# One expert's phi units loaded after its gathered rows and multiplied in its fourth step

## The chip, the cores and the metric

The kernel runs on one core of one Trainium2 chip. The metric is device time in microseconds (us) from the start to the end of one execution. Engines are named as the profile names them: PE (TensorE matmul), PEld (its weight loads), DVE (VectorE), ACT (ScalarE), POOL (GpSimd), SP (SyncE, which issues most DMAs). All data are float32.

## The reference

```python
state = gamma * state + k_t v_t^T; y_t = scale * q_t @ state      # retention, 4 x 8 heads, 768 steps
x = y as (3072, 512)
e_idx = argmax(x @ w_gate, 1)                                      # 8 experts, one for each token
ye = relu(x[mask_e] @ w1[e]) @ w2[e]                               # w1: 512x1024, w2: 1024x512
x = gate_w * sigmoid(x @ w_output_gate)[e] * ye                    # first mixture
logits = x @ phi                                                   # 32 slots
slot_in = softmax(logits, axis 0).T @ x ; slot_out = second mixture(slot_in)
out = softmax(logits, axis 1) @ slot_out
```

## The kernel before

Stage one (lines 312 to 718) computes retention tile by tile, writes the token rows to a DRAM table `xs` (lines 602 and 610) and sorts the tokens into eight lists, one for an expert. The experts are then taken in an order that the data decide; SP reads each expert's number into a register (`load_er`, line 195). Stage two (lines 834 to 1160) takes expert after expert, each in eight steps f of 128 hidden features; g counts all 64 steps. Stage three is the second mixture and the output.

Three streams of weights pass through SP, which issues in program order:

- W1: a step has a unit of 256 KB (`load_w`, line 207, three buffers `r`). ACT rounds it to `wh` (line 221) and DVE takes the rest, `wl` (line 222). In step g the unit of step g+3 is issued and the unit of step g+2 is split.
- phi units: w2 is never multiplied with the hidden rows for the logits; instead `wq_mm` (line 237) forms w2 times phi for an expert, 32 matmuls over four units q of 512 KB (`wq_load`, line 230, tile `wt`), and `wq_turn` (line 244) has DVE transpose the result to `wp`. `logits` (line 902) multiplies `wp` with the hidden rows `h`, first at f = 4 of the expert's own steps.
- `m2`: weights of the second mixture, fetched ahead into 21 places of 1024 columns (pool `m2p`, line 835; `load_m2`, line 1082, in every odd step from g = 5).

The place in question is the passage from stage one to stage two. At its end SP issues three W1 units and the four phi units of the first expert, two to a DMA of 1 MB (lines 677 to 680), into the buffers of stage one's input (`raw`). POOL gathers the first expert's 384 rows, in three DMAs of 128 rows, from `xs` into `xg` (line 704), as soon as the first list stands (lines 692 and 695). PE runs `wq_mm(0)` (line 687) and DVE `wq_turn(0)` into `pd` (line 718). Then every engine reads a number and branches past a block of code for experts with too many tokens (`If`, line 818; in this input the block is skipped). The first instruction after it on DVE is `x_scale(0, 0)` (line 852), which multiplies the gathered rows by their gate; PE transposes them (`x_mm`, line 861), ACT and DVE split the result to `xh` and `xl` (lines 870 and 871), and `l1` (line 883) runs a step: 12 matmuls.

SP's order after the branch is that of the code: the second expert's four phi units, held until the first gather has landed (lines 1049 to 1053), then step by step a W1 unit, m2 and the phi units for the expert after next. `wq_mm(1)` runs in step f = 4 of the first expert (`u = UMM + 2`, line 1094), later experts' in step f = 2.

```python
        for q in range(0, KD, 2):
            wq_load(0, q, 2, io, "raw")                  # 680
        wq_mm(0, pT, "w")                                # 687
        wq_turn(0, pd[:, 0:KF, :])                       # 718
        for q in range(KD):
            get = wq_load(1, q, 1, wup, "wu")            # 1051
            if q == 0:
                after(get, gets[0])
```

Of the kernel before, what the change touches and what calls it, by code (L numbers as in the profile page):

```python
# [9 lines left out]
F32 = mybir.dt.float32  # L10
# [12 lines left out]
E = 8  # L23
FF = 1024
NS = 32
NCH = S // 128
NTILE = NT // 128
KD = DM // 128
KF = FF // 128
# [6 lines left out]
CAP = NT + 256  # L36
NPRE, NX = 42, 4
NH = 6
IO, UMM = 6, 2
GROUPS = [(t, 3) for t in range(0, NTILE, 3)]  # L40
ENDS = {t + n - 1: (t, n) for t, n in GROUPS}
ORDER = "xe sc s m g1 gc xr rr g2 G0 Gb q oq os st G1 rk k".split()
# [95 lines left out]
def retention_moe_kernel(ctx, tc, qt, kt, kn, vn, gates, moe_w1, moe_w2,  # L138
# [50 lines left out]
    pd = per.tile([128, NBX, 32], F32, name="pd")  # L189
# [5 lines left out]
    def load_er(k):  # L195
        if k < E:
            er.append(nc.values_load(ordi[0:1, k:k + 1], engines=[mybir.EngineType.SP], min_val=0, max_val=E - 1))
# [9 lines left out]
    def load_w(g):  # L207
        if g >= G:
            return
        k, f = divmod(g, KF)  # L210
        t = wraw.tile([128, DM], F32, tag="r1", name="r1")
        nc.sync.dma_start(out=t, in_=moe_w1[bass.ds(er[k], 1), f:f + 1].rearrange("o q p c -> (o q p) c"))
        raw_t[g] = t
# [14 lines left out]
    wtt, wacc, wp = {}, {}, {}  # L228

    def wq_load(k, q, n, pool, tag):  # L230
        t = pool.tile([128, n * FF], F32, tag=tag, name="wt")
        get = nc.sync.dma_start(out=t, in_=moe_w2[1, bass.ds(er[k], 1), :, q * FF:(q + n) * FF].rearrange("o p d -> (o p) d"))
        for h in range(n):
            wtt[k, q + h] = [t[:, h * FF + g * 256:h * FF + g * 256 + 256] for g in range(4)]
        return get

    def wq_mm(k, pool, tag):
        wacc[k] = pool.tile([128, 256], F32, tag=tag, name="wps")
        for q in range(KD):
            for g, t in enumerate(wtt.pop((k, q))):  # L240
                nc.tensor.matmul(out=wacc[k][32 * g:32 * g + 32, :], lhsT=phi[:, q, :], rhs=t,  # L241
                                 start=(q == 0), stop=(q == KD - 1), skip_group_check=True)

    def wq_turn(k, out):
        wp[k] = out
        nc.vector.transpose(out=out, in_=wacc.pop(k).rearrange("p (f t) -> p f t", t=32))
# [65 lines left out]
    with ExitStack() as pa:  # L312
        sc2 = pa.enter_context(tc.tile_pool(name="sc2", bufs=2))
        io = pa.enter_context(tc.tile_pool(name="io", bufs=IO + 1))
        one = pa.enter_context(tc.tile_pool(name="one", bufs=1))
        pT = pa.enter_context(tc.tile_pool(name="pT", bufs=1, space=PSUM))
# [54 lines left out]
        raw, k2, q2, sps, sS, Ops, xT3, xr3, gps, gts, gs, scl, gr, oz = ({} for _ in range(14))  # L371
# [304 lines left out]
        load_er(0)  # L676
        for g in range(3):
            load_w(g)
        for q in range(0, KD, 2):
            wq_load(0, q, 2, io, "raw")  # L680
        rank(i)
        lp = pT.tile([128, 32], F32, tag="s", name="lp", bufs=2)
        nc.tensor.matmul(out=lp, lhsT=ones, rhs=base[:, 2, :], start=True, stop=False)
        for u in range(NTILE):
            for a in range(2):
                nc.tensor.matmul(out=lp, lhsT=lrow[:, u, :], rhs=lcol[:, u, a, :], start=False, stop=(a == 1 and u == NTILE - 1))
        wq_mm(0, pT, "w")
        lx = one.tile([128, E, 4, E], F32, name="lx")

        def lists(r):  # L690
            n = r.stop - r.start
            nc.vector.tensor_tensor(out=lx[:, r], in0=lp.rearrange("p (e j) -> p j e", j=4).unsqueeze(1).to_broadcast([128, n, 4, E]),
                                    in1=sq8[:, 0, r, :].unsqueeze(2).to_broadcast([128, n, 4, E]), op=ALU.mult)
            with nc.allow_low_precision(reason="a single whole number under 2 ** 24 among zeros"):
                nc.vector.tensor_reduce(out=xidx[:, r], in_=lx[:, r], axis=AX.X, op=ALU.add)
# [19 lines left out]
        nc.vector.tensor_reduce(out=lim[:, E:E + 1], in_=lim[:, 0:E], axis=AX.X, op=ALU.max)  # L715
        nc.vector.tensor_copy(out=limi, in_=lim)
        lists(slice(1, E))
        wq_turn(0, pd[:, 0:KF, :])

    whl = ctx.enter_context(tc.tile_pool(name="whl", bufs=3))  # L720

# [113 lines left out]
    m2p = ctx.enter_context(tc.tile_pool(name="m2p", bufs=NPRE // 2))  # L835
    hp = ctx.enter_context(tc.tile_pool(name="hp", bufs=NH))
    hbp = ctx.enter_context(tc.tile_pool(name="hbp", bufs=1))
    w2p = ctx.enter_context(tc.tile_pool(name="w2p", bufs=8))
    wup = ctx.enter_context(tc.tile_pool(name="wup", bufs=KD))
    with ExitStack() as pb:  # L840
        sp = pb.enter_context(tc.tile_pool(name="sp", bufs=1))
        ps_h = pb.enter_context(tc.tile_pool(name="ps_h", bufs=2, space=PSUM))
        ps_1 = pb.enter_context(tc.tile_pool(name="ps_1", bufs=1, space=PSUM))
# [173 lines left out]
        def slot_acc(e):  # L1017
            nc.vector.scalar_tensor_tensor(out=acc, in0=acc, scalar=sms.pop(e)[:, 4:5], in1=slo.pop(e), op0=ALU.mult, op1=ALU.add)
# [27 lines left out]
                load_w2(e, (2 * f - 6, 2 * f - 5))  # L1046

        load_er(1)
        for q in range(KD):

            get = wq_load(1, q, 1, wup, "wu")
            if q == 0:
                after(get, gets[0])
        for j in range(len(XT[0])):
            if j == 1:
# [6 lines left out]
        for g in range(G):  # L1062
            e, f = divmod(g, KF)
            if f == 0:
                load_er(e + 2)
            if e + 1 < E and f < len(XT[e + 1]):

                gather(e + 1, (f,))
                if f:
                    after(gets[e + 1][f], [relu[-1]])  # L1070
            split_w(g + 2)
            if e and f == 1:

                if e > 1:
                    slot_acc(e - 2)
                logit_parts(e - 1)
            if g < G - 3:
                load_w(g + 3)
            else:
                load_m2(wraw, "r1")  # L1080
            if g > 3 and g % 2 and len(m2_t) < NPRE:
                load_m2(m2p, "m2", 2)
            if f in (4, 5) and e + 1 < E:
                for j in range(2 * f - 8, min(2 * f - 6, len(XT[e + 1]))):
                    x_scale(e + 1, j)
            if f == KF - 1 and e + 1 < E:

                xps = x_mm(e + 1, "ABDr", sorted(((j, kk) for kk in range(KD) for j in range(len(XT[e + 1]))),
                                                 key=lambda b: XT[e + 1][b[0]] < 128))
                l1(g, lambda: [x_split(e + 1, ps) for ps in xps])  # L1090
            else:
                l1(g)
            behind(e - 1, f)
            u = UMM if e else UMM + 2
            if f == u and e + 1 < E:
                wq_mm(e + 1, ps_1, "A")
                wq_turn(e + 1, sp.tile([128, KF, NS], F32, tag="wp", name="wp", bufs=2))
            if f > u and f <= u + 3 and e + 2 < E:

                for q in ((0, 1), (2,), (3,))[f - u - 1]:  # L1100
                    wq_load(e + 2, q, 1, wup, "wu")
            elif G - 14 < g < G - 6 and f % 2:
                load_m2(wup, "wu", 2)
            if g == G - 6:
                load_w2(e, range(4), xp, "xy")
            if g >= G - 2:

                for i, tag in enumerate(("wh1", "wl1")):
                    load_w2(e, (2 * f - 8 + i,), whl, tag)
            if f == 4:  # L1110
                logits(e, 0)
            if f == 5:

                mask(e)
            if f >= 5:
                h_tr(e, 2 * f - 10)
                h_tr(e, 2 * f - 9)
        e = E - 1
# [30 lines left out]
        for kk in range(KD):  # L1149
            nc.tensor.matmul(out=ps4[:, kk, :], lhsT=acc[:, kk * 128:(kk + 1) * 128], rhs=sw,  # L1150
                             start=True, stop=True, skip_group_check=True)
# [171 lines left out]
```

## Time and profile before

| | |
|---|---|
| median of 3 runs | 437.55 us (435.31 to 442.07) |
| the profiled execution | 435.42 us |
| its span, first to last instruction | 433.6 us, so 1.8 us lie around it |
| mean granted PE clock | 0.948 of full |
| busy: PE, DVE, ACT, POOL | 377.8, 258.4, 162.2, 108.1 us |
| DMA | 130.88 MB, mean 302 GB/s |

Times in the rows are counted from the span's start. In the timeline a row gives start, length, engine, line, operation and tiles, and in brackets how long the engine was idle before and what ended that. SPq, DVEq and so on are the engines' queues of control instructions. Where the chain of waits names a DMA, its time runs from the issue to the landing.

### The profile page before, as it was taken

The page shows a single profiled execution, that of the slowest core. Times are in us where ns is not written, and L with a number is a line of the kernel's source. Part 1 is how long each engine was busy: PE and PEld are TensorE (multiplying, and loading weights), DVE is VectorE, ACT ScalarE, POOL GpSimd, SP SyncE. Part 2 cuts the span into 40 slices and gives each one's busy share as a digit, 9 for nine tenths or more (in the row PEclk, how much of TensorE's full clock was granted, in tenths as well). Part 3 has the DMA queues.
Part 4 walks back from the last instruction along what each step waited for, and adds up shares of the span by engine and source line. Part 5 has one row for each costly group of instructions (what it writes and reads, how often), then busy time and mean ns, then how long its engine had stood idle before and what let it go on. Part 6 is the DMA issues. An engine that isn't in the chain of part 4 may idle for free.

```text
span 433.6 us, 11468 instructions
## 1 busy us (share of the span) xinstructions
PE 377.8 (87%) x4398; PEld 285.2 (66%) x4398; DVE 258.4 (60%) x676; ACT 162.2 (37%) x359; POOL 108.1 (25%) x117
## 2 busy tenths in 40 slices
PE   2989999998335999999999999999999996799990
PEld 2877777786214897778777867877778873224560
DVE  1498889998604365595574765754766756424350
ACT  1432222222012644655454644635454431112242
POOL 2303333321120413143052241421521212020020
PEclk9999999999655999999999999999999999699996
DMA  8999999963587798988978979889577789999998
GB/s 268 381 425 347 288 322 322 324 162 76 119 304 247 238 360 300 381 273 295 390 248 303 380 267 346 298 275 377 166 253 278 257 281 289 390 384 408 397 365 291
DMA packets 66275, 130.88 MB, mean 302 GB/s; under 512 B 10436, under 2 KB 28866, under 8 KB 63650
## 3 DMA queue, kind: packets, MB, share of 16 engines
q1 hardware_dynamic: 59426, 118.07, 78.4%
q0 software_dynamic: 3344, 8.34, 6.3%
q10 hardware_dynamic: 3440, 3.63, 2.5%
q8 instruction: 37, 0.61, 0.6%
q14 instruction: 28, 0.23, 0.2%
HBM read 116.84 MB, written 13.20 MB: 300 GB/s over the span
## 4 chain that ended last, share of the span: by engine, by line
PE 72%; DVE 9%; DMA 7%; issue 4%; ACT 3%; another core or an unknown queue 2%; SPq 1%; ACTq 1%; POOL 0%; DVEq 0%; POOLq 0%
PE hps L883 31%; PE s L414 5%; PE gps L992 5%; PE o L447 4%; PE fh L1176 4%; PE so L1213 3%; PE wps L241 3%; DMA raw<-in_qt_dram 3%; DMA xg<-xs,xidx 3%; PE lps L909 3%; PE xps L861 2%; PE o L438 2%; PE slo L1014 2%; PE st L461 1%
## 5 line engine op out<-in xcount | busy, mean ns | idle before, releaser
L883 PE MATMUL hps<-xh,wh 128*128 128x416 f32 (+2 forms) x256 | 92.0, 360 | 0.1
L883 PE MATMUL hps<-xl,wh 128*128 128x416 f32 (+2 forms) x256 | 88.9, 347 | 0.0
L883 PE MATMUL hps<-xh,wl 128*128 128x416 f32 (+2 forms) x256 | 88.7, 346 | 0.0
L222 DVE TENSOR_TENSOR wl<-r,wh 128x512 fp32r<-128x512 f32 x64 | 43.3, 677 | 43.6 <-ACT wh L221 41.2
L888 ACT ACTIVATE h<-hps 128x416 f32<-128x416 f32 (+2 forms) x64 | 32.7, 511 | 81.6 <-PE hps L883 75.9
L883 PEld LDWEIGHTS hps<-xh,wh 128*128 128x128 f32 x256 | 48.1, 188 | 15.1 <-issue 11.4
L975 POOL DMA_INDIRECT ctok<-ce,xidx x29 | 29.2, 1009 | 99.9 <-DVE ce L972 93.5
L221 ACT ACTIVATE wh<-r 128x512 fp32r<-128x512 f32 x64 | 40.0, 628 | 26.4 <-DMA r<-in_moe_w_dram 13.4
L883 PEld LDWEIGHTS hps<-xl,wh 128*128 128x128 f32 x256 | 48.2, 188 | 0.9 <-DVE xl L871 0.3
L883 PEld LDWEIGHTS hps<-xh,wl 128*128 128x128 f32 x256 | 48.1, 188 | 0.6
L704 POOL DMA_INDIRECT xg<-xs,xidx x29 | 29.9, 1031 | 65.3 <-ACT h L888 42.1
L424 DVE TENSOR_TENSOR sS<-s,csa 128x512 f32<-128x512 f32 x48 | 30.5, 675 | 16.3 <-PE s L414 16.3
L414 PE MATMUL s<-raw 64*128 64x128 f32 x384 | 32.5, 305 | 8.7 <-DMA raw<-in_qt_dram 8.3
L414 PEld LDWEIGHTS s<-raw 64*128 64x128 f32 x384 | 27.1, 204 | 11.5 <-DMA raw<-in_qt_dram 5.5
L895 DVE STREAM_TRANSPOSE hB<-h 128x416 f32<-128x416 f32 (+2 forms) x64 | 34.4, 576 | 0.0
L447 PE MATMUL o<-sS,raw 128*64 128x128 f32 x384 | 27.5, 288 | 0.0
L396 POOL TENSOR_TENSOR k<-raw,cs 128x512 f32<-128x512 f32 x20 | 22.3, 1132 | 17.0 <-DMA raw<-in_qt_dram 14.7
L479 ACT COPY xT<-o 128x512 f32<-128x512 f32 x24 | 13.9, 580 | 32.9 <-PE o L447 32.9
L241 PE MATMUL wps<-wt,phi 128*32 128x256 f32 x256 | 17.4, 414 | 9.0 <-DMA wt<-in_moe_w_dram 7.2
L447 PEld LDWEIGHTS o<-sS,raw 128*64 128x64 f32 x384 | 21.6, 142 | 3.9 <-issue 3.6
L992 PE MATMUL gps<-hB,pd 32*32 32x256 f32 x816 | 20.1, 405 | 3.7 <-DVE pd L946 3.7
L870 ACT ACTIVATE xh<-xps 128x416 fp32r<-128x416 f32 (+2 forms) x32 | 16.0, 513 | 14.8 <-DMA wt<-in_moe_w_dram 8.4
(174 smaller groups left out, 525.2 us busy)
## 6 DMA issues: line engine op xcount, KB each, us to landing
m<-in_moe_w_dram SPq DMA_DIRECT2D x41, 512.0 KB
r<-in_moe_w_dram SPq DMA_DIRECT2D x64, 256.0 KB
w<-in_moe_w_dram SPq DMA_DIRECT2D x64, 256.0 KB
wt<-in_moe_w_dram SPq DMA_DIRECT2D x28, 512.0 KB
m<-in_moe_w_dram SPq DMA_DIRECT2D x36, 256.0 KB
xs<-xr SPq DMA_DIRECT2D x32, 192.0 KB
raw<-in_kt_dram SPq DMA_DIRECT2D x5, 1024.0 KB
raw<-in_kn_dram SPq DMA_DIRECT2D x5, 1024.0 KB
```

The lines of the kernel that those rows point to most:

```text
L221: nc.scalar.activation(out=hi, in_=t, func=ACTF.Copy)
L222: nc.vector.tensor_tensor(out=lo, in0=t, in1=hi, op=ALU.subtract)
L241: nc.tensor.matmul(out=wacc[k][32 * g:32 * g + 32, :], lhsT=phi[:, q, :], rhs=t, start=(q == 0), stop=(q == KD - 1), skip_group_check=True)
L414: nc.tensor.matmul(out=ps[h][:, p, :], lhsT=kq(i, p, 0)[r], rhs=kq(i, p, 1)[r], start=True, stop=True, tile_position=(64 * h, 0), skip_gro ...
L424: nc.vector.tensor_tensor(out=sS[i][:, h], in0=sps.pop((i, h)), in1=con("dm", 128)[:, 4 * h:4 * h + 4, :], op=ALU.mult)
L447: nc.tensor.matmul(out=o_at(i, p, h), lhsT=vals(i, 2 * p + h), rhs=s[:, h, p, :], start=(i % NCH == 0 and n < 4), stop=True, skip_group_ch ...
L704: gets.setdefault(e, []).append(nc.gpsimd.indirect_dma_start(out=t[0:r, :], out_offset=None, in_=xs[:, :], in_offset=bass.IndirectOffsetOn ...
L883: nc.tensor.matmul(out=ps, lhsT=a[:, kk * 128:(kk + 1) * 128], rhs=x[e][kk][:, 0:c], start=(n == 0), stop=(n == 11))
L888: relu.append(nc.scalar.activation(out=hs[g][:, 0:c], in_=ps, func=ACTF.Relu))
L895: nc.vector.transpose(out=hB[e][:, 0:NB[e], f, :], in_=hs[e * KF + f][:, 0:c].rearrange("p (b t) -> p b t", t=32))
L975: put = nc.gpsimd.indirect_dma_start(out=ctok[:, :], out_offset=bass.IndirectOffsetOnAxis(ap=xidx[0:r, e, j:j + 1], axis=0), in_=cn[0:r, j ...
L992: nc.tensor.matmul(out=ps[a][32 * j:32 * j + 32, :], lhsT=pd[q, b, :], rhs=hB[e][q, b].rearrange("p f t -> p (f t)"), start=(i == 0), stop ...
```

## The change

The first expert's phi units leave stage one. They are issued after the branch, one DMA a unit, into four of the m2 places, the first held until the first gather has landed, where the second expert's units stood. The second expert's are issued one a step in the first four steps. `wq_mm(0)` and `wq_turn(0)` stand after the matmuls of step f = 3 of the first expert, `wq_mm(1)` after those of f = 5 (before: f = 4). For later experts the fourth unit is issued with the third, one step earlier. `QA` is 0, so that all four units are taken.

```diff
-        for q in range(0, KD, 2):
-            wq_load(0, q, 2, io, "raw")
         rank(i)
...
-        wq_mm(0, pT, "w")
...
         lists(slice(1, E))
-        wq_turn(0, pd[:, 0:KF, :])
...
-        for q in range(KD):
-
-            get = wq_load(1, q, 1, wup, "wu")
-            if q == 0:
+        for q in range(QA, KD):
+
+            get = wq_load(0, q, 1, m2p, "m2")
+            if q == QA:
                 after(get, gets[0])
...
             behind(e - 1, f)
-            u = UMM if e else UMM + 2
+            if e == 0 and f < KD - QA:
+                wq_load(1, QA + f, 1, wup, "wu")
+            if e == 0 and f == 3:
+                wq_mm(0, ps_1, "A")
+                wq_turn(0, sp.tile([128, KF, NS], F32, tag="wp", name="wp", bufs=2))
+            u = UMM if e else 5
             if f == u and e + 1 < E:
                 wq_mm(e + 1, ps_1, "A")
                 wq_turn(e + 1, sp.tile([128, KF, NS], F32, tag="wp", name="wp", bufs=2))
-            if f > u and f <= u + 3 and e + 2 < E:
-
-                for q in ((0, 1), (2,), (3,))[f - u - 1]:
+            if f in (u + 1, u + 2) and e + 2 < E:
+
+                for q in ((0, 1), (2, 3))[f - u - 1]:
                     wq_load(e + 2, q, 1, wup, "wu")
```

On SP, at the end of stage one, before the change: r1 are the W1 units, wt the phi units, limi the number that decides the branch.

```order
L212 DMA r1_1643<-in_moe_w1_dram 128x512
L212 DMA r1_1645<-in_moe_w1_dram 128x512
L212 DMA r1_1647<-in_moe_w1_dram 128x512
L232 DMA wt_1649<-in_moe_w2_dram 128x2048
L232 DMA wt_1651<-in_moe_w2_dram 128x2048
L727 TENSOR_LOAD limi_81
L818 COMPARE_AND_BRANCH
```

The same place after the change (the lines have moved up by four):

```order
L212 DMA r1_1643<-in_moe_w1_dram 128x512
L212 DMA r1_1645<-in_moe_w1_dram 128x512
L212 DMA r1_1647<-in_moe_w1_dram 128x512
L723 TENSOR_LOAD limi_81
L814 COMPARE_AND_BRANCH
```

The two DMAs of 1 MB are gone from in front of the branch.

On SP, from the first DMA after the branch, before the change: wt_3499 to wt_3505 are the second expert's phi units.

```order
L232 DMA wt_3499<-in_moe_w2_dram 128x1024
L232 DMA wt_3501<-in_moe_w2_dram 128x1024
L232 DMA wt_3503<-in_moe_w2_dram 128x1024
L232 DMA wt_3505<-in_moe_w2_dram 128x1024
L197 TENSOR_LOAD ordi_79
L212 DMA r1_3568<-in_moe_w1_dram 128x512
L212 DMA r1_3593<-in_moe_w1_dram 128x512
L212 DMA r1_3618<-in_moe_w1_dram 128x512
L212 DMA r1_3643<-in_moe_w1_dram 128x512
```

The same place after the change: wt_3477 to wt_3483 are the first expert's units, wt_3563 to wt_3644 the second's.

```order
L232 DMA wt_3477<-in_moe_w2_dram 128x1024
L232 DMA wt_3479<-in_moe_w2_dram 128x1024
L232 DMA wt_3481<-in_moe_w2_dram 128x1024
L232 DMA wt_3483<-in_moe_w2_dram 128x1024
L197 TENSOR_LOAD ordi_79
L212 DMA r1_3546<-in_moe_w1_dram 128x512
L232 DMA wt_3563<-in_moe_w2_dram 128x1024
L212 DMA r1_3573<-in_moe_w1_dram 128x512
L232 DMA wt_3590<-in_moe_w2_dram 128x1024
L212 DMA r1_3600<-in_moe_w1_dram 128x512
L232 DMA wt_3617<-in_moe_w2_dram 128x1024
L212 DMA r1_3627<-in_moe_w1_dram 128x512
```

Four units stand in front of the fourth step's W1 unit as before, but each of the next W1 units now has a phi unit in front of it.

## Rows read from the trace of the kernel before

**Rows 1.** The page, the span in 40 equal slices: PE and DMA in tenths.
```profile
PE   2989999998335999999999999999999996799990
DMA  8999999963587798988978979889577789999998
```
**Rows 2.** The page, the costliest group: busy, mean ns of one, idle before.
```profile
L883 PE MATMUL hps<-xh,wh 128*128 128x416 f32 (+2 forms) x256 | 92.0, 360 | 0.1
```
**Rows 3.** The chain of waits, 117 to 139 us: start, length, what.
```profile
118.24 11.44 DMA xg<-xs,xidx
...
130.16 1.52 SPq L232
...
131.88 5.62 DMA wt<-in_moe_w_dram
...
137.62 0.50 ACT xh L870
```
**Rows 4.** The timeline, 116 to 145 us, engine by engine (PE, DVE, ACT, POOL).
```profile
128.38 1.94 PE L241 MATMUL wps<-wt,phi 128*32 128x256 f32 x16 [1.72 <-SPq L818]
135.30 2.79 PE L861 MATMUL xps<-cs,xg 128*128 128x128 f32 x12 [4.99 <-DVE xg L852]
...
119.42 0.39 DVE L695 TENSOR_REDUCE xidx<-lx 128x28 int32<-128x224 f32 x1
130.38 0.45 DVE L246 STREAM_TRANSPOSE pd<-wps 128x256 f32<-128x256 f32 x1 [10.58 <-PE wps L241]
134.56 0.49 DVE L852 TENSOR_SCALAR xg<-xg 128x512 f32<-128x512 f32 x1 [3.72 <-DVEq L818]
...
141.10 0.49 ACT L888 ACTIVATE h<-hps 128x384 f32<-128x384 f32 x1 [0.81 <-PE hps L883]
143.18 0.49 ACT L888 ACTIVATE h<-hps 128x384 f32<-128x384 f32 x1 [1.07 <-PE hps L883]
...
121.16 1.01 POOL L704 DMA_INDIRECT xg<-xs,xidx  x1 [0.30 <-issue]
```
**Rows 5.** Line 818, the branch: ns min/median/max, first and last start in us.
```profile
L818 SPq EVENT_SEMAPHORE  x9: 17/17/17, 125.8 to 128.6; - x9
...
L818 ACTq EVENT_SEMAPHORE  x2: 17/17/17, 125.3 to 125.4; - x2
...
L818 DVEq EVENT_SEMAPHORE  x2: 21/21/21, 134.3 to 134.4; - x2
L818 ACTq COMPARE_BRANCH  x1: 50/50/50, 119.7 to 119.7; - x1
...
L818 DVEq COMPARE_BRANCH  x1: 72/72/72, 131.0 to 131.0; - x1
```
**Rows 6.** A later gather alone: its issue (POOL's timeline), and queue 0, 165.6 to 167.6.
```profile
163.60 1.01 POOL L704 DMA_INDIRECT xg<-xs,xidx  x1 [4.38 <-ACT h L888]
...
q0 software_dynamic: 74, 0.25, 42.9%
```
**Rows 7.** The chain of waits from 138 us: steps 0 to 4, then wq_mm(1).
```profile
138.16 11.22 PE hps L883 x60
149.38 1.86 PE wps L241 x32
```
**Rows 8.** Stretches of 4 us: busy (x) by engine, granted PE clock, DMA share, GB/s.
```profile
120.00:124.00 4.00, 0.00 (x0) 0.00 (x0) 0.00 (x0) 0.00 (x0) 1.87 (x2) 0.50 0.99 356
...
128.00:132.00 4.00, 1.94 (x16) 0.60 (x16) 0.45 (x1) 0.72 (x1) 1.01 (x1) 0.50 0.37 95
132.00:136.00 4.00, 0.70 (x4) 0.73 (x5) 1.44 (x3) 0.00 (x0) 0.00 (x0) 0.50 0.85 301
136.00:140.00 4.00, 3.93 (x17) 3.23 (x16) 1.94 (x5) 2.38 (x6) 0.00 (x0) 0.62 0.81 283
140.00:144.00 4.00, 4.00 (x25) 4.00 (x24) 1.99 (x4) 2.13 (x5) 1.07 (x2) 1.00 0.51 161
...
156.00:160.00 4.00, 4.00 (x30) 3.73 (x29) 2.30 (x5) 2.39 (x5) 1.09 (x1) 1.00 1.01 392
```
**Rows 9.** Tile r, the W1 units: what ended ACT's and DVE's idle time, us, times.
```profile
  DMA r<-in_moe_w_dram: 13.4, 11
```

More of the change, by code (lines that the diff above doesn't have):

```diff
@@ L38 @@
 NH = 6
-IO, UMM = 6, 2
+IO, UMM, QA = 6, 2, 0
 GROUPS = [(t, 3) for t in range(0, NTILE, 3)]
@@ L238, in wq_mm @@
         wacc[k] = pool.tile([128, 256], F32, tag=tag, name="wps")
-        for q in range(KD):
+        for q in range(QA, KD):
             for g, t in enumerate(wtt.pop((k, q))):
                 nc.tensor.matmul(out=wacc[k][32 * g:32 * g + 32, :], lhsT=phi[:, q, :], rhs=t,
-                                 start=(q == 0), stop=(q == KD - 1), skip_group_check=True)
+                                 start=(q == QA), stop=(q == KD - 1), skip_group_check=True)
     def wq_turn(k, out):
@@ L838, in retention_moe_kernel @@
     w2p = ctx.enter_context(tc.tile_pool(name="w2p", bufs=8))
-    wup = ctx.enter_context(tc.tile_pool(name="wup", bufs=KD))
+    wup = ctx.enter_context(tc.tile_pool(name="wup", bufs=KD - QA))
     with ExitStack() as pb:
@@ L1048, in retention_moe_kernel @@
         load_er(1)
-        for q in range(KD):
-            get = wq_load(1, q, 1, wup, "wu")
-            if q == 0:
+        for q in range(QA, KD):
+            get = wq_load(0, q, 1, m2p, "m2")
+            if q == QA:
                 after(get, gets[0])
```

## The prediction

> **What bounds the kernel now.** I read the page's slices first: PE is at nine tenths nearly everywhere, with a hole of three slices about 108 to 141 us and a weaker tail [rows 1]. Inside the expert loop PE waits for nothing: the costliest matmul group has 0.1 us of idle time before it in 256 instructions [rows 2]. So an edit in the loop costs what it adds to PE, unless transfers fall behind, and what the change can win lies in the hole.
>
> The chain of waits through the hole comes next [rows 3]. From 118.24 it lies on the gathers, 11.44 us until all have landed at 129.68; then on SP and the second expert's phi units, and at 137.62 on ACT's first `xh`. Its last releaser, the phi units, is not to be believed: `xh` needs the transposes, and the timeline has them begin at 135.30, released by DVE's scaling of 134.56 [rows 4]. That scaling has 3.72 us of idle time before it, ended by DVE's own branch, and before that 10.58 us in which DVE stood on `wq_turn(0)`. So the true path before 137.62 is: phi units land, second half of `wq_mm(0)` at 128.38, `wq_turn(0)` at 130.38, branch, scaling, transposes.
>
> The branch by itself: ACT compares at 119.7 and runs its first instruction on the skipping path at 125.3, 5.6 us later; DVE compares at 131.0 and is there at 134.3, 3.3 us [rows 5]. Nothing in the program is waited for in between. ACT's wait falls into a stretch with a DMA share of 0.99, DVE's into one that begins at 0.37 and rises to 0.85 [rows 8]. [...]
>
> **The change part by part.** *What goes at the front.* DVE has nothing left before the branch after the lists, which end at 119.42 + 0.39 = 119.81. With the compare at 120.4 at the latest, 3.3 us and the 0.2 us from 134.4 to 134.56, the first scaling stands at 123.9 instead of 134.56: 10.7 us earlier. With ACT's 5.6 us in place of the 3.3 it stands at 126.2, 8.4 us earlier.
>
> The rows must be there too. Two MB of phi units no longer share the engines with the gathers. A later gather, issued at 163.60 among other traffic, has its packets done by 167.6 at the latest, 4.0 us [rows 6]; the third gather is issued at 121.16 [rows 4], so it lands by about 125.2, and its scaling ends about 125.7. PE starts on the first rows at 124.6 (135.30 is 0.74 us after 134.56) and reaches the third rows only after eight of its twelve transposes, 8/12 of 2.79 = 1.9 us, at 126.5: the third gather is covered. The end of the path, 2.32 us from 135.30 to 137.62, is the same. Bounds: gathers as late as now (129.68) put the third scaling's end at 130.2 and the ninth transpose with `xh` at 130.4, which leaves 7.2 us of gain; a compare 0.2 us earlier, right behind the lists, gives 10.9. I take 10.5 us, near DVE's row, less 0.2 us for five engines branching together.
>
> *What comes on PE.* `wq_mm(0)` now ran in PE's idle time and moves between steps 3 and 4. The row of `wq_mm(1)` at full clock gives 1.86 us for 32 matmuls [rows 7]; the half-clock one takes 1.94 us for 16 [rows 4], so 3.9 us is the upper end. It is 1.9 us, with nothing beside it to hide it. `wq_mm(1)` only changes its step. `wq_turn(0)` waits on DVE for PE as the others do; behind it is `wl` of two steps later: nothing.
>
> *The clock.* It is granted at 0.50 until 136, 0.62 on average to 140, and 1.00 from 140 [rows 8]: PE's stream began at 135.30. After the change it begins at 124.6 without the two bursts of `wq_mm(0)` before it. If the rise comes as long after the start, nothing is lost; from -0.3 to +1.7 us (one step at half clock), I take 0.3 us.
>
> *The new wait on SP.* The first unit waits for the gathers (about 125.2) and for the branches of the other engines. Behind it on SP stand three units, a register load and the fourth W1 unit. Before, from the first unit's issue at 130.16 to the last landing at 137.50 it took 7.34 us [rows 3]; issue at 125.4 gives 132.7 for all four. The W1 unit behind them, 256 KB at 349 GB/s (283 at a share of 0.81, [rows 8]), lands about 133.5 and is split to `wh` by 134.2 and `wl` by 135.0. Steps are 2.08 us apart (141.10 to 143.18), the first took 2.94 us from 138.16 to 141.10 [rows 4, 7]; with `l1` starting at 127.7 step 3 is due at 127.7 + 2.94 + 2 x 2.08 = 134.8. So it is just in time, and phi itself is not needed before 136.9.
>
> Then each step asks for a W1 unit, a phi unit and a gather, 0.26 + 0.52 + 0.27 = 1.05 MB, 3.0 us at 349 GB/s against a step of 2.08. From the first unit (126) to the second expert's last there are 6.2 MB: 17.8 us, 143.8; `wq_mm(1)` is due after step 5, at 136.9 + 1.9 + 2 x 2.08 + 0.7 (logits) = 143.7. Again just in time. At 392 GB/s (the best row) nothing waits; at 300 it is 3 us late. I take 1.0 us for these waits together. Afterwards the demand is that of before, and the backlog is worked off where the share was under 1.
>
> *Later experts.* The fourth unit now stands ahead of the W1 unit of f = 5, which lands 0.52 MB / 349 = 1.5 us later. ACT already waits for W1 units in 11 places, 13.4 us together [rows 9], and PE does not feel it [rows 2]. I take 0; if every one of five experts lost all of it, 7.5 us, if an earlier issue saved the waits, up to -1. The m2 places are 21, the first four wanted again only by the eighteenth load, step 39: nothing.
>
> **Sum**: -10.5 + 1.9 + 0.3 + 1.0 = -7.3 us, 435.42 - 7.3 = 428.1 in the terms of the profiled execution. That execution is near the lowest of the three runs, 2.1 us under the median; a median of a few runs should lie about half of that above it, so I predict 429.0.
>
> **The rivals.**
> 1. *Nothing is given back*: transfers run at 392 GB/s, the clock rises as before. -10.9 + 1.9 = -9.0 us: 426.4. For it: the best row; against it: gathers and units mixed never reached it here.
> [...]
> 3. *The gathers are slow by themselves*: the rows land at 129.7 whatever the phi units do. The front gives 7.2 us; the units start as late as now, so that the fourth W1 unit lands at 138.2 and step 3 waits 1.4 us: -7.2 + 1.9 + 0.3 + 1.4 + 1.0 = -2.6, 432.8. Against it: the later gather's 4.0 us.
> [...]
>
> **How the numbers follow.** Forecast 0.48 (own range 426.5 to 431), rival 1 0.25, rival 2 0.15, rival 3 0.08, rival 4 0.04. Two per cent, about what a measurement of this kernel can tell from no change, is 8.7 us. Faster by more: most of rival 1 and a tail of the forecast, 0.36. Slower by more: part of rival 4, 0.03. Within: 0.61. The range 424.5 to 435 holds the first three cases and rival 3, with the scatter of the runs; what is left out is rival 4 and the ends.
>
> **What would show it.** Right: DVE's first scaling at about 124 with an idle time of 3 to 4 us ended by its branch; `xh` at 127; 32 wps matmuls of 1.9 us after the fourth step; the hps row's idle time still near 0.1. Wrong: a branch of 5 us or more on DVE (rival 2), the scaling ended by DMA xg after 128 (rival 3), PE idle on `wh` or `wt` in the first expert and a clock of 0.50 beyond 131 (rival 4), or ACT waiting for W1 units much longer than 13.4 us in all.

## The result and the profile after

The changed kernel took 433.91 us (median, 430.9 to 439.3) beside 438.78 us (434.9 to 443.81) of the kernel before on the same chip: ratio 0.9905, 95% interval 0.9882 to 0.9928, a gain of 4.2 us (0.0095 x 438.78). Run twice more in the experiments, it gave 0.9858 (0.981 to 0.9906) and 0.987 (0.9813 to 0.9926), 6.2 and 5.7 us. The forecast was 429.0 after 437.55, a gain of 8.5. The profiled execution took 432.81 us (435.42 before), its span 431.0 (433.6); 1.23 us of that is stage one, which ended earlier by chance: the first gather was issued at 117.01 instead of 118.24. Below, times are therefore also counted from that issue. In stage two the line numbers are those of before less 4.

The page after, PE and DMA in 40 slices, to be laid beside [rows 1]:

```profile
PE   2889999998249999999999999999999996799990
DMA  7999999953569999988979889799577789999988
```

PE's hole is one slice shorter, and in the four slices behind it DMA stands at nine throughout, where it had 7, 7, 9 and 8. The page's row of the costliest group answers to [rows 2]:

```profile
L879 PE MATMUL hps<-xh,wh 128*128 128x416 f32 (+2 forms) x256 | 92.7, 362 | 0.6 <-ACT h L884 0.5
```

The chain of waits of the kernel after, 117 to 164 us (start, length, what), answers to [rows 3, 7]:

```profile
117.01 7.64 DMA xg<-xs,xidx
...
127.73 6.81 DMA r<-in_moe_w_dram
...
134.63 0.63 ACT wh L221
135.26 0.39 ACT h L884
...
135.69 2.38 PE hps L879 x12
138.07 1.86 PE wps L241 x32
...
145.33 1.86 PE wps L241 x32
...
150.20 8.44 DMA r<-in_moe_w_dram
...
158.73 0.64 ACT wh L221
...
160.08 0.48 DVE ll L913
...
160.60 0.44 PE lsum L926
```

Before, the chain behind `xh` was PE alone, matmul after matmul. Now it leaves PE twice, each time for a W1 unit (tile `r`): the one for the first expert's fourth step, and the one for the second expert's fourth step. The latter is split two steps ahead, and behind that split ACT and DVE form `ls` and `ll`, for whose sums (`lsum`) PE waits. The phi units (`wt`) are not in it: they come in time, and what stands behind them on SP comes late.

The timelines of DVE, ACT and PE and the rows of the branch (line 814, was 818) answer to [rows 4, 5]:

```profile
118.19 0.39 DVE L692 TENSOR_REDUCE xidx<-lx 128x28 int32<-128x224 f32 x1
123.48 0.49 DVE L848 TENSOR_SCALAR xg<-xg 128x512 f32<-128x512 f32 x1 [4.91 <-DVEq L814]
...
126.54 1.64 ACT L866 ACTIVATE xh<-xps 128x384 fp32r<-128x384 f32 x4 [2.38 <-PE xps L857]
...
135.69 0.45 PE L879 MATMUL hps<-xh,wh 128*128 128x384 f32 x1 [0.53 <-ACT h L884]
```

```profile
L814 DVEq EVENT_SEMAPHORE  x2: 21/21/21, 123.3 to 123.4; - x2
L814 ACTq COMPARE_BRANCH  x1: 50/50/50, 118.4 to 118.4; - x1
...
L814 DVEq COMPARE_BRANCH  x1: 72/72/72, 118.8 to 118.8; - x1
```

The scaling no longer waits for `wq_turn(0)`: DVE compares at 118.8, 0.2 us after its last list has ended (118.19 + 0.39), and stands on the branch for 4.5 us. Stretches of 4 us (busy by engine, granted clock, DMA share, GB/s) answer to [rows 8]:

```profile
124.00:128.00 4.00, 3.71 (x14) 3.03 (x15) 1.95 (x4) 1.61 (x5) 1.01 (x1) 0.50 0.45 123
128.00:132.00 4.00, 4.00 (x18) 4.00 (x18) 2.21 (x5) 1.70 (x4) 0.23 (x1) 0.73 1.01 383
132.00:136.00 4.00, 3.47 (x21) 3.14 (x19) 0.69 (x1) 1.01 (x2) 0.88 (x2) 1.00 1.03 398
...
144.00:148.00 4.00, 4.00 (x45) 2.82 (x44) 1.71 (x4) 3.25 (x7) 0.00 (x0) 1.00 0.89 271
148.00:152.00 4.00, 4.00 (x30) 3.73 (x29) 2.97 (x6) 1.75 (x5) 0.65 (x1) 1.00 0.98 342
152.00:156.00 4.00, 4.00 (x25) 3.50 (x27) 3.47 (x7) 2.98 (x6) 0.44 (x1) 1.00 0.99 378
156.00:160.00 4.00, 3.64 (x21) 2.42 (x21) 1.83 (x5) 1.82 (x4) 1.01 (x1) 1.00 1.01 390
```

From 128 to 160 us the DMA engines are full, but for the stretch from 144 to 148, and PE, which was busy throughout this stage before, is not: 3.47 and 3.64 of 4 where the two waits lie. The sum over tile `r` (what ended ACT's idle time, us, times) answers to [rows 9], 13.4 us in 11 places before:

```profile
  DMA r<-in_moe_w_dram: 25.3, 18
```

For one number per part, three stretches are taken from the timelines of each trace: the front (first gather's issue to the first `xh`), the middle (first `xh` to the fourth expert's `wps`, the phi multiplication in the third expert) and the rest (to the first `fh`).

| kernel (trace) | front | middle | front + middle | rest | ratio to before |
|---|---|---|---|---|---|
| before | 19.38 | 61.27 | 80.65 | 179.54 | |
| before again (E6) | 24.09 | 61.18 | 85.27 | 178.44 | 1.0004 |
| E3, before + later experts' part | 20.94 | 62.24 | 83.18 | 177.12 | 0.9986 |
| after | 9.53 | 66.86 | 76.39 | 182.25 | 0.9905 |
| after again (E5) | 9.22 | 67.28 | 76.50 | 178.52 | 0.9858 |
| after again (E11) | 9.70 | 68.43 | 78.13 | 176.08 | 0.987 |
| E1, later experts as before | 9.45 | 66.79 | 76.24 | 173.81 | 0.9842 |
| E2, second expert's units gone | 9.71 | 65.34 | 75.05 | 175.03 | 0.9795 |
| E4, W1 unit first | 9.44 | 65.62 | 75.06 | 178.75 | 0.9788 |
| E12, W1 unit first again | 9.92 | 64.82 | 74.74 | 176.25 | 0.983 |
| E7, matmuls to warm up | 11.03 | 65.47 | 76.50 | 180.54 | 0.9849 |
| E8, E4 and E7 together | 10.98 | 63.61 | 74.59 | 178.52 | 0.9806 |
| E9, one phi unit for eight | 9.57 | 63.84 | 73.41 | 173.85 | 0.9772 |
| E10, E9 with 8 of 32 matmuls | 9.55 | 63.00 | 72.55 | 175.52 | 0.9755 |

Before has 61 to 62 us in the middle, after 67 to 68. The rest scatters by 6 us over three traces of one and the same kernel (after, E5, E11), so nothing is read from it below. In the profiled pair it took 2.7 us more after the change (182.25 beside 179.54). In the chains of after and E5 four waits of 1.5 to 2.4 us in it are put down to another core or an unknown queue, and such waits stand in the chain of before too; E11 has none.

### The profile page after: what moved, and what is told of

Its sections match the earlier page's. It is cut to its first block, busy times and chain, and to the rows that moved or that the text cites. A ratio compares the mean times of both kernels' runs of the same rounds, so it can differ in the third digit from the quotient of the medians.

```text
span 431.0 us, 11475 instructions
## 1 busy us (share of the span) xinstructions
PE 377.8 (88%) x4398; PEld 283.9 (66%) x4398; DVE 256.9 (60%) x676; ACT 161.6 (37%) x359; POOL 108.1 (25%) x117
## 3 DMA queue, kind: packets, MB, share of 16 engines
HBM read 116.84 MB, written 13.20 MB: 302 GB/s over the span
## 4 chain that ended last, share of the span: by engine, by line
PE 63%; DMA 12%; DVE 11%; issue 4%; ACT 4%; another core or an unknown queue 2%; SPq 1%; ACTq 1%; POOL 0%; DVEq 0%; POOLq 0%
PE hps L879 25%; DMA r<-in_moe_w_dram 5%; PE s L414 4%; PE gps L988 4%; PE fh L1177 4%; PE o L447 4%; PE wps L241 3%; PE so L1214 3%; DMA raw<-in_qt_dram 3%; PE o L438 2%; PE slo L1010 2%; DVE hB L891 2%; PE lps L905 2%; DMA xg<-xs,xidx 2%
## 5 line engine op out<-in xcount | busy, mean ns | idle before, releaser
L221 ACT ACTIVATE wh<-r 128x512 fp32r<-128x512 f32 x64 | 40.1, 628 | 36.7 <-DMA r<-in_moe_w_dram 25.3
L701 POOL DMA_INDIRECT xg<-xs,xidx x29 | 29.8, 1029 | 61.2 <-ACT h L884 41.9
L414 PE MATMUL s<-raw 64*128 64x128 f32 x384 | 31.4, 299 | 9.9 <-DMA raw<-in_qt_dram 9.9
L414 PEld LDWEIGHTS s<-raw 64*128 64x128 f32 x384 | 26.2, 198 | 12.5 <-DMA raw<-in_qt_dram 5.7
L857 PE MATMUL xps<-cs,xg 128*128 128x128 f32 (+2 forms) x116 | 15.5, 284 | 8.8 <-ACT xg L850 8.0
L857 PEld LDWEIGHTS xps<-cs,xg 128*128 128x128 f32 (+2 forms) x116 | 13.1, 149 | 12.5 <-ACT xg L850 8.0
```

The costliest lines, as they stand in the source:

```text
L221: nc.scalar.activation(out=hi, in_=t, func=ACTF.Copy)
L414: nc.tensor.matmul(out=ps[h][:, p, :], lhsT=kq(i, p, 0)[r], rhs=kq(i, p, 1)[r], start=True, stop=True, tile_position=(64 * h, 0), skip_gro ...
L701: gets.setdefault(e, []).append(nc.gpsimd.indirect_dma_start(out=t[0:r, :], out_offset=None, in_=xs[:, :], in_offset=bass.IndirectOffsetOn ...
L857: nc.tensor.transpose(out=ps[kk][:, j * 128:j * 128 + r], in_=xg[e][j][0:r, kk * 128:(kk + 1) * 128], identity=ident[0:r, 0:r])
```

## The experiments

Each ratio is to the kernel before on the same chip. E1 to E4 ran on one chip, E5 to E8 on a second, E9 to E12 on a third.

**E1: the later experts' units as before.** Of the change, only the pair of the last two units goes.

```
-            if f in (u + 1, u + 2) and e + 2 < E:
-                for q in ((0, 1), (2, 3))[f - u - 1]:
+            if f > u and f <= (u + 3 if e else u + 2) and e + 2 < E:
+                for q in (((0, 1), (2,), (3,)) if e else ((0, 1), (2, 3)))[f - u - 1]:
```

> The changed kernel, but from the second expert on the fourth phi unit is issued a step after the third again, as before the change. Transfer theory (a W1 unit with one more phi unit ahead of it lands late and is on the path, in the third expert at 208.5 us): 1.1 to 1.5 us faster than the changed kernel, ratio to before about 0.987, and the wait of ACT for the W1 unit at 208.5 us is gone or under 1 us. Rival (the later experts cost nothing, the loss is on PE in the first expert): ratio stays at 0.990.

Measured: 429.02 us, ratio 0.9842 (0.9788 to 0.9895). Beside 0.9905, 0.9858 and 0.987 for the changed kernel this is no difference that the runs can tell: the intervals overlap. The wait for a W1 unit at 208 us is gone from its chain, but it is gone from E11's too, which has the new order.

E1's trace shows something else. The clock rose early in it: the first step, from its first matmul to that of the second step, took 2.76 us, as in the kernel before (2.74) and not 3.72 as in the result's trace. Yet the middle is the same, 66.79 beside 66.86, because PE waited longer ahead of the fourth step, 1.72 us in place of 0.53, as E1's timeline of PE shows:

```profile
135.88 0.45 PE L879 MATMUL hps<-xh,wh 128*128 128x384 f32 x1 [1.72 <-ACT h L884]
```

ACT began to split the fourth step's W1 unit 17.7 us after the first gather's issue in E1 and 17.6 in the result's trace. That landing, and not PE's speed before it, sets the fourth step.

**E3: the later experts' part alone, on the kernel before.**

```
-            if f > u and f <= u + 3 and e + 2 < E:
-                for q in ((0, 1), (2,), (3,))[f - u - 1]:
+            if f > u and f <= (u + 2 if e else u + 3) and e + 2 < E:
+                for q in (((0, 1), (2, 3)) if e else ((0, 1), (2,), (3,)))[f - u - 1]:
```

> The kernel before, with one part of the change alone: from the second expert on the fourth phi unit is issued with the third. Transfer theory: about 1.1 us slower than before, ratio 1.002 to 1.003, with ACT waits for W1 units longer than 13.4 us in all. Rival (this part costs nothing): ratio 1.000, waits as before.

Measured: 435.4 us, ratio 0.9986 (0.9946 to 1.0026). By itself this part costs at most 1.1 us (0.0026 x 437.06). ACT waits 16.8 us for W1 units in place of 13.4, as the theory said, but no wait of PE in the middle comes of it. With E1 this part is not what took the gain.

**E2: the second expert's phi units not loaded**; the first expert's stand in their place, so the second expert's scores are other numbers.

```
-            if e == 0 and f < KD - QA:
-                wq_load(1, QA + f, 1, wup, "wu")
             if e == 0 and f == 3:
+                for q in range(KD):
+                    wtt[1, q] = wtt[0, q]
```

> The changed kernel without the second expert's four phi units: its product is formed from the first expert's units once more, so the second expert's logits are those of other weights. 2 MB less in the first expert's steps, all PE work stays. Transfer theory: the fifth to eighth W1 unit land 1.4 us and more earlier, the second expert's PE stall at 159 to 160 us goes; from the first hps matmul to the third expert's phi multiplication 34.6 us instead of 36.4; ratio to before about 0.986. The stall before the fourth step stays, since its W1 unit is still behind the first expert's units. Rival (PE's moved multiplication, the clock and the broken stream are the loss): 36.4 us as in the changed kernel, ratio 0.990.

Measured: 427.33 us, ratio 0.9795 (0.9745 to 0.9845). The chain loses the second of its two W1 waits and keeps the first (7.05 us of DMA `r` in place of 6.81), ACT waits 16.1 us for W1 units instead of 25.3, and the middle is 65.34. From the first `hps` matmul to the third expert's `wps` it has 34.8 us in place of 36.3, close to the theory's 34.6. So the transfers of the second expert's units cost 1.5 us there beside the result's trace, 1.9 and 3.1 beside those of E5 and E11. The ratio is lower than the 0.986 foretold, which the middle alone does not explain.

**E4: the same loads in another order.** The fourth step's W1 unit goes ahead of the first expert's phi units, the second expert's units come one step later behind the next W1 unit and are multiplied in step 7; later experts are as before, the third expert's in two pairs.

```
-        for q in range(QA, KD):
-            get = wq_load(0, q, 1, m2p, "m2")
...
+            if g == 0:
+                for q in range(KD):
+                    wq_load(0, q, 1, m2p, "m2")
...
-            if e == 0 and f < KD - QA:
-                wq_load(1, QA + f, 1, wup, "wu")
+            if e == 0 and 1 <= f <= KD:
+                wq_load(1, f - 1, 1, wup, "wu")
...
-            u = UMM if e else 5
+            u = {0: 7, 1: 3}.get(e, UMM)
```

> The changed kernel in another order of transfers: the fourth step's W1 unit is issued ahead of the first expert's phi units, each of the second expert's units behind the W1 unit of the next step; the second expert's product moves to the eighth step, the third's to the fourth step of the second expert, and from the second expert on units are issued as before the change. Same work, same bytes. Transfer theory: no stall before the fourth step (0.6 us less), none for the W1 unit at 158.7 us, none at 208.5 us; 3 us faster than the changed kernel, ratio to before about 0.984. Rival (the loss is PE's own): ratio 0.990.

Measured: 428.03 us, ratio 0.9788 (0.9742 to 0.9835), middle 65.62. Nothing is left out, and by the interval the kernel is 1.7 to 2.6% faster than the one before; the theory had 0.984. PE still waits 0.4 and 1.0 us in the first expert, and the chain still has 9.59 us of DMA `r` from 133.01, so transfers bind here too. ACT's wait for W1 units is 26.6 us, longer than the 25.3 of the changed kernel with its longer middle: that sum alone does not tell what PE loses.

**E5: the changed kernel again.**

> The changed kernel as it is, beside the kernel before on one chip, for a trace taken under the same conditions as those of E1 to E4. Theory (half of the loss behind the front comes from transfers in the first expert, the rest from the later experts' fourth phi unit ahead of a W1 unit): ratio 0.988 to 0.993 to the kernel before, that is 4 to 5 us above E1 and E2 on the scale of the kernel before; the phi units' landing for the third expert is followed by a wait of ACT for the fourth W1 unit of about 8 us in the chain, and the third expert's wps comes at 46.4 us after the first gather's issue, 1.3 us later than in E2. Rival (the difference between the result and E1, E2 is that of the chips or of the hour, not of the parts): ratio 0.980 to 0.984, that of E1 and E2, and a trace with 29.3 us per expert as E1 to E4 have.

Measured: 432.4 us, ratio 0.9858, just between theory and rival. The wait for a W1 unit that the theory placed behind the third expert's phi units is not there; one of 8.09 us of DMA `r` comes at 230.96, an expert later. That the later experts take half of the loss is thus not borne out. The third expert's `wps` came at 46.51 as foretold. Ahead of the fourth step PE waits 1.56 us, for a W1 unit that ACT began to split 18.1 us after the first gather's issue. The first W1 unit in the chain of waits of E5 is the next one, for the fifth step:

```profile
130.95 9.49 DMA r<-in_moe_w_dram
...
152.52 7.81 DMA r<-in_moe_w_dram
```

**E6: the kernel before again.**

> The kernel before beside itself: the scatter of the method, and a trace under the same conditions as those of the experiments. Theory: ratio 1.000 with an interval of about 0.003 to either side; first expert's xh about 19.4 to 20.9 us after the first gather's issue (19.38 in the trace of before, 20.94 in E3). If xh comes at 20.9, the front gave the change 11.4 us and not 9.9, and what was given back behind it is larger by 1.5 us. Experts 29.3 us apart as in E1 to E4 would say that the 29.96 us of the first two traces belong to the run; 29.96 that the later experts of E1, E2 and E4 really gained 0.6 us each.

Measured: ratio 1.0004 (0.9969 to 1.004). Its front is 24.09 us, beyond both values named. The rows of its branch, then its timeline of DVE:

```profile
L818 DVEq EVENT_SEMAPHORE  x2: 21/21/21, 138.6 to 138.7; - x2
...
L818 DVEq COMPARE_BRANCH  x1: 72/72/72, 132.8 to 132.8; - x1
```

```profile
132.15 0.45 DVE L246 STREAM_TRANSPOSE pd<-wps 128x256 f32<-128x256 f32 x1 [12.82 <-PE wps L241]
138.80 0.48 DVE L852 TENSOR_SCALAR xg<-xg 128x512 f32<-128x512 f32 x1 [6.20 <-DVEq L818]
```

The branch takes DVE 5.8 us here instead of 3.3 [rows 5], and `wq_turn(0)` comes at 132.15 although the gathers were issued 0.47 us earlier. Of the 4.7 us by which this front is longer, the branch makes 2.5, and 2.2 lie ahead of `wq_turn(0)`. In E3 the branch takes 4.0 us (131.6 to 135.6). The kernel before thus has a front of 19.4, 20.9 or 24.1 us, the changed one 9.2 to 9.7: the change gave 9.9 us in the profiled pair and up to 14.9 between other traces. In the three traces of the changed kernel the branch takes DVE 4.2 to 4.5 us. As to the distance between experts: from the fourth expert's `wps` to the seventh's it is 29.8 to 30.0 us here, but 29.3 to 29.4 in E1 and E2 and also in E11, the changed kernel itself. So this difference belongs to the run and not to the parts.

**E7: matmuls on resident data to raise the clock**, 8 ahead of the branch, 5 behind it, results unused.

```
+        wm = pT.tile([128, 128], F32, tag="w", name="wm")
+        for _ in range(8):
+            nc.tensor.matmul(out=wm, lhsT=ident, rhs=ident, start=True, stop=True)
...
+        wm2 = ps_h.tile([128, 128], F32, tag="h", name="wm2")
+        for _ in range(5):
+            nc.tensor.matmul(out=wm2, lhsT=ident, rhs=ident, start=True, stop=True)
         xps = x_mm(0, "ABCD", ...
```

> The changed kernel with 8 matmuls of 128x128 on resident data ahead of the branch and 5 behind it, ahead of the first transposes, whose results nothing reads. In the changed kernel the transposes and most of the first step ran at a granted clock of 0.50, the clock rose about 6 us after the stream began; the first step took 3.72 us against 2.94 in the kernel before. Theory (the clock takes 0.8 us or a little more of what the front gave): the clock is 1.00 some 1 to 2 us earlier, the transposes or the first step are 0.5 to 1.5 us shorter, ratio to the kernel before 0.986 to 0.990 where the changed kernel has 0.990. Rival (the first expert is bound by its transfers, so what the clock gives back is waited for in step 3): the first step shrinks, the wait for the fourth W1 unit grows by as much, ratio as E5. Second rival (the five matmuls behind the branch delay the transposes): xh later than in E5, ratio higher.

Measured: 433.29 us, ratio 0.9849 (0.9802 to 0.9896). E7's timeline of PE (with two records for each of the five matmuls), then its stretches of 2 us:

```profile
125.58 2.47 PE L1059 MATMUL wm<-cs 128*128 128x128 f32 x10 [3.62 <-DVEq L817]
127.85 2.77 PE L860 MATMUL xps<-cs,xg 128*128 128x128 f32 x12
```

```profile
128.00:130.00 2.00, 2.00 (x12) 2.00 (x11) 0.00 (x0) 0.00 (x0) 1.01 (x1) 0.50 0.57 121
130.00:132.00 2.00, 1.78 (x8) 1.13 (x8) 1.34 (x3) 1.86 (x5) 0.00 (x0) 0.87 1.03 389
```

The matmuls held up the transposes, as the second rival said: the front is 1.8 us longer than in E5. The clock was 0.50 from 128 to 130 and 0.87 on average from 130 to 132, so by estimate it rose at 130.5 us, 2.7 us into the transposes, and the first step took 2.62 us in place of E5's 3.48, as the theory had it. (The text above sets 3.72 us against 2.94, which counts to ACT's first `h`; counted alike the kernel before has 2.74.) That the matmuls brought the rise forward is not shown: it came 11.4 us after the first gather's issue, and 10.6 to 14.6 us after it in the traces of the changed kernel and its variants without them, by the lengths of the `hps` matmuls (in E11, the latest, 0.52 us before the rise and 0.34 after).

The 1.8 us were made up by the shorter first step (0.86) and a shorter wait ahead of the fourth (0.71 in place of 1.56, so 0.85). Front and middle together are 76.50 us in both, though E11 with 78.13 shows that the agreement to the hundredth is chance, and the ratio is that of E5. ACT began to split the fourth step's W1 unit 18.2 us after the first gather's issue, and 18.1 in E5. As long as that unit sets the fourth step, a front 1.8 us shorter is worth nothing.

**E8: E4 with E7's matmuls.**

> E4 (W1 unit of the fourth step ahead of the first expert's phi units, second expert's units one step later behind the next W1 unit) with the 8 and 5 matmuls of E7. Theory: E4 took the transfers off the first expert's path, so what the clock gives shows in the end: 0.5 to 1.5 us under E4, ratio 0.976 to 0.978. Rival (PE's stream waits for something else there, such as the first W1 parts or the second step's): ratio as E4, 0.979.

Measured: 430.51 us, ratio 0.9806 (0.976 to 0.9852). Not under E4: the rival holds, and front and middle together (74.59) are again those of the kernel without the matmuls (75.06, 74.74). The first step is shorter (2.64 us, 3.17 in E4), and so are PE's waits in the middle (0.4 us in all, 1.4 in E4).

**E9: one phi unit loaded in place of eight.**

```
+            if q > QA:
+                wtt[0, q] = list(wtt[0, QA])
+                continue
             get = wq_load(0, q, 1, m2p, "m2")
...
-                wq_load(1, QA + f, 1, wup, "wu")
+                wtt[1, QA + f] = list(one_unit)
```

> The changed kernel with one phi unit in place of eight for the first two experts: the first expert's units 1 to 3 and the second expert's four are not loaded, unit 0 is multiplied in their place (the scores of those two experts are thereby other numbers). All matmuls stay. From the first xh to the wps of the fourth expert the two traces of the kernel before have 61.2 us, the changed kernel 66.9 and 67.3, E2 65.3. Theory (of the 5.7 to 6.1 us given back, 1.9 are the multiplication, 0.8 the clock, the rest transfers): 63.5 to 64.5 us in this stretch, ACT's wait for W1 units at most E2's 16.1 us, ratio 0.973 to 0.978. Rival (what E2 left is not transfers, but a first expert that runs at the low clock or waits between ACT, DVE and PE): 65.3 us as in E2 and ratio 0.979.

Measured: 425.94 us, ratio 0.9772 (0.972 to 0.9824), middle 63.84, ACT's wait for W1 units 13.1 us. The chain of waits from the first `xh` of E9:

```profile
127.06 9.26 PE hps L879 x48
136.31 1.86 PE wps L241 x32
138.18 2.30 PE hps L879 x12
140.48 0.78 PE lps L905 x8
141.26 2.31 PE hps L879 x12
143.57 1.86 PE wps L241 x32
145.44 2.30 PE hps L879 x12
```

It is PE alone, as in [rows 7], with the added 1.86 us of `wps`. All values are where the theory had them.

**E10: E9 with 8 of the 32 matmuls of the first expert's phi multiplication** (units 1 to 3 left out of the product).

```
+        qs = [QA] if k == 0 else list(range(QA, KD))
-        for q in range(QA, KD):
+        for q in qs:
```

> E9 with the first expert's phi multiplication cut from 32 matmuls to 8 (its units 1 to 3 are left out of the product). Theory (the multiplication lies wholly on PE's path): 1.4 us less than E9 from the first xh to the fourth expert's wps, ratio 0.003 under E9. Rival (PE has idle time nearby, on wh or on the scores, that takes the multiplication up): less than 0.5 us, same ratio.

Measured: 424.63 us, ratio 0.9755 (0.9701 to 0.9809), middle 63.00, 0.84 us less than E9. The `wps` group takes 0.64 us in place of 1.93, and from it to the second expert's `wps` there are 5.97 us (19.72 to 25.69 after the gather) in place of 7.25 (19.31 to 26.56): 1.28 us, the whole of what was taken off. The other 0.4 us were lost ahead of it, in the first step, which the edit does not touch: it took 3.30 us in place of 2.85, with a granted clock of 0.50 from 128 to 129 us beside 0.92 in E9. So the multiplication lies on PE's path; the ratio alone could not have told it.

**E11 and E12: the changed kernel and E4 on one chip.**

> The changed kernel once more, as the yardstick of E9, E10 and E12 on their chip. E5 gave 0.986 (0.981 to 0.991), the result 0.9905 (0.988 to 0.993). Theory (both are one value, and the kernel before is what scatters, since its branch on DVE waits between 3.3 and 5.8 us): 0.986 to 0.991, xh 9.2 to 9.6 us after the first gather's issue. Rival (the ratio belongs to the chip): a value outside.

> E4 once more, beside the changed kernel on one chip. Theory (the order of the transfers in the first expert is worth 2 to 5 us): ratio 0.977 to 0.983, and 0.005 to 0.011 under E11. Rival (E4's lead belongs to its chip; E8 had 0.9806 beside E5's 0.9858, with intervals that overlap): within 0.003 of E11.

Measured: 0.987 (0.9813 to 0.9926) and 0.983 (0.9776 to 0.9883). The kernel with the W1 unit first beats the kernel before in both of its runs, and its middle is 1.2 to 3.6 us shorter than that of the changed kernel in every pair of traces. That it beats the changed kernel in total time is likely and not shown: 0.004 lies inside both intervals.

## Why the prediction was wrong

**The front (forecast -10.5 us): right in kind, 0.65 us too much.** In the profiled pair it gave 9.85 (19.38 to 9.53). The first scaling had the branch as its releaser, as foretold, 6.5 us after the first gather's issue (123.48 less 117.01) where the forecast had 5.7 (123.9 less 118.24), and the gathers landed by 124.65. DVE's stall was 4.5 us, not the 3.3 of [rows 5]; the compare came 0.4 us sooner after the lists than assumed. Rival 2 (the branch stays at 5.6) did not happen, nor did rival 3 (late gathers). That DVE's 3.3 us would come, and not ACT's 5.6, was the author's estimate, and so were the 0.2 us taken off for five engines branching together, which no run shows. In the result's trace the five compare at 118.4 to 118.8, and DVE's stall is 1.2 us longer than in [rows 5]. What DVE waits for there is not shown. In the trace of before the DMA queue q14, of kind `instruction`, has one packet in DVE's stall (131.0 to 134.4), in that of the changed kernel five, beside one of q8, of the same kind (118.8 to 123.3). DVE's longest stall, 5.8 us in E6, falls into stretches with a DMA share of 0.88 and 0.83 (132 to 140), and in the changed kernel 4.5 us fall into one of 0.66 (120 to 124). But the share does not order all cases: 3.3 us was measured where it rose from 0.37 to 0.85 [rows 5, 8].

**The phi multiplication (+1.9): right.** 1.93 us in the trace, and on the path by E10.

**The clock (+0.3): too small, but it cost nothing of its own.** The first step took 3.72 us in the result's trace and 2.74 before, 1.0 us more, and 3.48 and 4.28 in E5 and E11: a scatter that was not foreseen. But E1, with 2.76, has the same middle, because PE then waits longer for the fourth step's W1 unit. Beside the multiplication E9, in which PE has no waits, gives back 63.84 - 61.27 - 1.93 = 0.6 us. Its first step accounts for 0.1 of that (2.85 beside 2.74); the other 0.5 is not assigned.

**The waits of the first expert (+1.0), and the sentence "afterwards the demand is that of before, and the backlog is worked off where the share was under 1": this step failed.** The loss to transfers is the middle less that of E9: 66.86 - 63.84 = 3.0 us in the result's trace, 3.4 in E5, 4.6 in E11. These differences hold the late clock too, but E1, whose first step is as short as E9's, has 66.79 - 63.84 = 3.0 as well. Once the transfers flowed, the rate was not the error: the forecast used 349 GB/s, and the stretches from 128 to 140 show 383 to 398, about its best row, at which it had said that nothing waits.

Two things were wrong. The first is the landing of the fourth step's W1 unit. The forecast put it 15.3 us after the first gather's issue (133.5 less 118.24) and called it just in time; it came at 17.5 (127.73 + 6.81 less 117.01). Of the 2.3 us, 0.8 lie ahead of the issue of the first phi unit (124.95) and 1.5 between that issue and the landing, 9.6 us in place of 8.1: from 125 to 128 us the engines moved only 25, 164 and 303 GB/s, microsecond by microsecond. PE was ready at 135.16 and waited 0.5 us, since ACT handles `h` behind `wh`.

The second is that for the steps behind it the forecast asked only when the phi units land, and they were in time. The W1 units that stand behind them on SP were not asked after, and the backlog was not worked off. Over 42 us from the same point before `xh`, the DMA engines moved 13.20 MB where they had moved 12.20 before. Before, they stood already at shares of 0.81, 0.86, 0.94 and 1.01 in the four stretches from 144 to 160, which leaves some 1.6 us of full engines, by estimate 0.6 MB at 390 GB/s, for 1.0 MB more. So a W1 unit is late a second time (issued at 150.20), and E2 takes that wait away. E7 says the same from the other side: with `xh` 1.8 us later the fourth step begins 19.2 us after the first gather's issue, and 19.1 in E5.

The prediction's own signs of being wrong in this came: ACT's wait for W1 units was 25.3 us beside 13.4, and the idle time of the `hps` row 0.6 us beside 0.1.

With these, 9.9 gained, 1.9 + 0.6 + 3.0 = 5.6 given back (66.86 - 61.27), and 4.3 left (80.65 - 76.39) in front and middle of the profiled pair. That the ratio gives 4.2 as well is luck: in the same pair the rest took 2.7 us more, of which some 1.1 us lie at one W1 wait of the third expert and the cause of the others is open, and stage one 1.2 us less. Between E6 and E5, on one chip, front and middle left 8.8 us, and the ratio gives 6.2.

**The later experts (0): not contradicted.** E3 allows 1.1 us at most on the kernel before; E1 is not told apart from the changed kernel. The profiled execution shows one wait of 8.29 us of DMA `r` in the third expert, with about 1 us lost on PE, but waits of this kind come in E4's trace too, which has the old order there, and are absent from E11's, which has the new one.

**The step from the profiled execution to the median** added 0.9 us for an execution 2.1 us under its own median, so that a gain of 7.3 became one of 8.5. A forecast of the median should have kept the difference. The rivals' times lack these 0.9 us, so they stand on another scale than the forecast's 429.0. On that scale rival 3 is at 433.7, next to the measured 433.91, but by chance: its mechanism, gathers that land at 129.7, did not occur.

None of the rivals came. Rival 4 (a first expert that starves and stays at a clock of 0.50) was right in that the first expert starves, but in the result's trace the granted clock was 1.00 in every stretch of 4 us from 132 to 164, also in those with PE's waits, and the DMA engines moved 271 to 398 GB/s from 128 to 160; PE's waits in the middle are 0.4 to 1.6 us each in the three traces of the changed kernel.

## What to carry to other kernels

When loads are moved out of an idle stretch into a busy one, do not test the moved load against its own deadline alone; test each load that stands behind it in the queue, and carry the backlog on, stretch by stretch, until the trace of before shows real slack. Where it will be late, order the issues by when their data is due: here the W1 unit ahead of the phi units gave back a part of what the change had lost (a middle of 64.82 and 65.62 us in place of 66.86 to 68.43). And when a wait is removed at the front, ask whether the time behind it still begins there: delaying the front by 1.8 us cost nothing in E7, so shortening it further would gain nothing while the W1 unit sets the fourth step.

## What had not been expected of the hardware

- The same branch, never taken into its body, stalls DVE by 3.3, 4.0 and 5.8 us in three traces of one front (before, E3, E6), and by 3.8 to 4.7 in the traces of the changed kernel and its variants (E4, E12), in which all engines compare within 0.5 us of each other.
- With the same stream of transposes and matmuls, the granted clock rose from 0.50 to 1.00 some 4 us after the stream began in E9 (124.12; 0.96 from 128 to 130), 6 us in the result's trace (124.23; 0.73 from 128 to 132) and 7 us in E11 (126.33; 0.54 from 132 to 134). That extra matmuls ahead of it bring it forward is not shown (E7).
- Gains made early can be lost at the end: from `fh` to the end of the program the changed kernel takes 55.2 to 55.4 us in its three traces, but E1, E9 and E10, which come there earlier, 57.7 to 59.7, with second-layer weights (DMA `m`) in their chains. The next bound may stand there; but E2, as early as E1 and with the same loads in its chain, takes 55.8.
